# Sliding-window attention with key tiles shifted by half a tile

## The chip, the core and the metric

The kernel runs on one core of a Trainium2 chip: a matrix engine (TensorE, PE in the profile; its weight loads are PEld), a vector engine (VectorE, DVE), an activation engine (ScalarE, ACT), a general engine (GpSimd, POOL), a queue engine that issues DMAs (SyncE, SP), and 16 DMA engines. The metric is the device time of one execution in microseconds; lower is better.

## The reference

Two layers, each an attention block and a gated feed-forward block, on 2048 tokens of width 512, in bfloat16:

```python
def _A_ref(x, wqkv, wo):
    B, S, D = x.shape
    H = 32; Dh = D // H; W = 256
    qkv = (x @ wqkv).reshape(B, S, 3, H, Dh).transpose(2, 0, 3, 1, 4)
    q, k, v = qkv[0], qkv[1], qkv[2]
    scores = jnp.einsum("bhqd,bhkd->bhqk", q, k) * (Dh ** -0.5)
    idx = jnp.arange(S)
    mask = (idx[:, None] - idx[None, :] >= 0) & (idx[:, None] - idx[None, :] < W)
    scores = jnp.where(mask[None, None], scores, -1e9)
    p = _softmax(scores, axis=-1)
    o = jnp.einsum("bhqk,bhkd->bhqd", p, v)
    return o.transpose(0, 2, 1, 3).reshape(B, S, D) @ wo

def _B_ref(x, w_gate, w_up, w_down):          # widths 512, 1792
    return (_sigmoid(x @ w_gate) * (x @ w_up)) @ w_down

x = A_x
for _ in range(2):
    x = x + _A_ref(_layernorm(x), A_wqkv, A_wo)
    x = x + _B_ref(_layernorm(x), B_w_gate, B_w_up, B_w_down)
```

A query sees itself and the 255 tokens before it. There are 32 heads of 16 channels.

## The kernel before

**Layout and stages.** Tokens come in 16 tiles of 128 (`NT`), four to a group (`NBG`). For a tile: a layer norm on VectorE and POOL (`layer_norm`), a transpose into `xnT` (by TensorE for the first tiles, otherwise by a DMA), units of TensorE work for Q, K (a group at a time, `q_unit` L695, `k_unit` L726) and V (a tile at a time, `v_unit` L765), scores, exponentials, masks and values, a second transpose, the output projection (`oproj_unit` L889), and the feed-forward units (`glu_units` L790, `down_units` L851). The two layers run into each other: as soon as the tokens that a tile needs are there, its next stage may begin.

**The attention.** With a window of 256 and tiles of 128, the keys of a tile j concern six 64-token query units, 2j to 2j+5. The four in the middle are scored for all 128 keys (an A visit, four per tile, one for each eight heads: `scores` L1029, two quads of 256 columns). Of unit 2j only the first half of the keys counts, of 2j+5 only the second; a fifth visit R scores those two half-tile pieces (L1040, 8 quads of 64 columns; half as many for the last two tiles of a layer). The last tile has one S visit (L1050) in place of the A visits. Scores of a visit fill the four PSUM banks `Sps`; one exp on ScalarE empties them (L1082, 2048 columns) into `PTring` (nine 64-column units per head, placed by the table `UNIT`) or `edge`. VectorE multiplies the triangular pieces by a mask (L960).

The probabilities lie with the keys on the partitions. `values` (L1084) multiplies them with V, which carries a column of ones per head for the sum of the softmax: 32 output rows for each head, so that four heads (a quad of matmuls) share the 128 columns of the array. For a half tile (16 heads, one bank) and each of four columns of heads, a tile from t=2 on takes one quad of 128 columns from key tile t-1 and four quads of 64 columns: from t-2, from t, and from two copies `Vl` and `Vh` in which the half tiles of V for the edges stand next to each other, zero-padded to 128 rows (made by DMAs, `half_values` L1303). Rows of a token tile are stored interleaved (row 2k+z is token 64z+k), which the loads, the moves of Q and of the values, and the stores undo or make.

The result of a half is moved by VectorE or ScalarE from its bank to `OTs` (`after_values` L1115, L668), then transposed by a DMA to `Oq`, normalised, transposed again, and projected.

**The order.** It is written out ahead by a planner (`Plan`, L168), which replays a model of the chip and hands each engine its instructions in the order in which the model begins them. `pick` (L1206) decides what TensorE does next: a visit when its exp slot and its pace (`PACE`) allow it; values when all their masks, V and a free bank are there, and when TensorE is not in a dense run; otherwise `choose` (L1344) picks among the open dense units and the heads of the streams by `rank`. There are four free banks (`BANKS`) for dense units and values; `choose` keeps the last one free when the next values are due. A unit holds its bank until its eviction has run. VectorE and ScalarE tasks are taken by the priorities in `PRIO` and `LATE_PRIO`. An exp waits until the values that still read its ring units are done (`ring_free`, L930: the values of t-1, same half).

Of the kernel before, what the change touches and what calls it, by code (L numbers as in the profile page):

```python
# [12 lines left out]
P = 128  # L13
# [11 lines left out]
VW = H * VS + 32  # L25
UNITS = 9
# [8 lines left out]
UNIT = [  # L35
    (4, 5, 7, 8), (1, 2, 3, 4), (0, 1, 5, 6), (2, 3, 7, 8), (0, 1, 4, 5), (7, 2, 3, 6), (0, 1, 7, 8), (2, 3, 4, 5),
    (1, 2, 6, 7), (1, 3, 4, 0), (1, 2, 5, 6), (3, 4, 7, 8), (0, 1, 2, 3), (4, 5, 6, 7), (0, 1, 2), (8,),
    (3, 4, 5, 6), (0, 1, 7, 8), (2, 3, 4, 5), (1, 2, 6, 7), (1, 3, 4, 0), (1, 2, 5, 6), (3, 4, 7, 8), (1, 2, 3, 0),
    (4, 5, 6, 7), (1, 2, 3, 4), (0, 1, 5, 6), (2, 3, 7, 8), (0, 1, 4, 5), (2, 3, 6, 7), (0, 1, 2), (8,),
]  # L40


# [14 lines left out]
def pool_ns(n):  # L57
# [5 lines left out]
GLU = [[[1] * 4 + [4], [1] * 4 + [2] * 2, [1] * 6 + [2], [1] * 8, [2] * 4, [1] * 2 + [2] * 3, [2] * 2 + [4]], [[4] * 3 + [2, 1, 1], [4] * 3 + [2, 2], [4] * 4]]  # L63
PACE = [2682, 3207, 1600, 2511, 23.52]
EARLY = 12
# [16 lines left out]
PRIO = dict(st_x0=7.13, ap_x0=2.72, xt_x0=3.36, st_x1=-0.44, ap_x1=1.86, xt_x1=6.58, st_x=18.87, ap_x=6.56,  # L82
    xt_x=2.0, st_p=7.13, ap_p=4.46, xt_p=0.81, st_g=2.23, ap_g=1.32, xt_g=6.14, st_g0=5.97, ap_g0=3.21,
    xt_g0=1.33, tp=5.75, tp_g=-0.06, q=4.0, q0=5.51, q1=4.74, k=1.95, k0=-0.89, k1=-1.49, s=-1.15, s0=5.46,
    s1=3.28, v=0.28, v0=5.43, v1=14.72, vv=5.53, exp=3.64, exp0=4.71, m0=4.61, m00=-0.56, e0=1.11, e00=1.28,
    e1=7.21, e10=6.56, m2=0.64, m20=3.6, th=5.12, mu=-0.12, dn=1.29, add=-0.27, add0=1.8, out=-2.4, mv=5.8,
    mv0=6.23, oq=-2.27, oq0=-0.14, no=4.71, no0=2.61, on=5.93, on0=0.59, vc=9.2, vc0=-0.87)
OPT = dict(gu='SP', g1=1, bk=3, bq=2, wide=0, r0=2, g0=1, g2=1, x0=1, eps=1, hold=0, own=1, ck=0, cq=2,
    turn=2)
SLACK = dict(xt=1208, oq=843, on=211, vc=1208)  # L90
RANK = dict(tp=-1.708, o=-2, lead=14.747, far=7.411, v=9.3, g=1.778, d=1.823, feed=11.672, x3=21097, wd=474,
    go=364)
LATE_PRIO = dict(st_p=-0.04, ap_p=7.96, xt_p=-0.99, st_x=1.07, ap_x=4.81, xt_x=-1.16, st_g=1.75, ap_g=1.19,
    xt_g=2.76, q=3.84, k=4.33, s=4.05, v=0.61, exp=1.12, m0=4.62, e0=2.79, e1=4.39, m2=5.49, th=1.65, mu=2.51,
    dn=2.1, add=0.69, out=0.45, mv=3.49, oq=0.77, no=6.44, on=2.16, vc=0.22)
LATE_SLACK = dict(xt=489, oq=1327, on=2346, vc=897)
LATE_RANK = dict(tp=-2, o=1.576, lead=9.722, far=6.159, v=1.796, g=1.769, d=3.896, feed=7.551, go=1418)
# [271 lines left out]
class Net:  # L369


    def __init__(self, ctx, tc, A_x, wqkv, wo, w_gate, w_up, w_down, out):
# [24 lines left out]
        self.kTp = big.tile([P, NCQ, KS, 2, P], BF16, name="kTp")  # L397
        self.Vaug = [big.tile([P, 2, VW], BF16, name=f"Vaug{i}") for i in range(VP)]
        self.hT = big.tile([P, HCH * GW], BF16, name="hT")
        self.ring = big.tile([P, H, UNITS, HP], BF16, name="PTring")  # L400
        self.edge = big.tile([P, 5, H // 2, HP], BF16, name="edge")
        self.Vd = [[big.tile([P, 2, VW], BF16, name=f"V{'lh'[z]}{i}") for i in range(2)] for z in range(2)]
# [4 lines left out]
        self.odd = [big.tile([P, 1], F32, name=f"odd{z}") for z in range(2)]  # L407
# [9 lines left out]
        ring("xn", 2, [P, 2, D])  # L417
        ring("xnT", 3, [P, NBG, KT, P])
# [25 lines left out]
    def loads(self, A_x, wqkv, wo, w_gate, w_up, w_down):  # L444
# [12 lines left out]
        def load_x(dst, tiles, n, prio=2, queues=("SP", "SP"), after=0):  # L457
            done, parts = Event(), []
            for z in range(2):
                src = A_x[0].rearrange("(t z k) d -> z k t d", z=2, k=HP)[z][:, tiles, :]  # L460
                parts.append(load(dst[z:P:2], src, n * HP * D * 2, after, prio, queues[z], 780))
# [42 lines left out]
    def constants(self):  # L504
# [12 lines left out]
        for i in range(2):  # L517
            self.zeros(0, i)
# [1003 lines left out]
```

The softmax here doesn't subtract the row's maximum and nothing guards it: scores larger than these inputs give would overflow.

## Time and profile before

| what | us |
|---|---|
| median of 3 runs | 541.5 (540.59 to 541.67) |
| profiled execution, first to last instruction | 539.6 |
| dense matmuls of 512 columns of L862 (434) and L798 (560), mean of one | 0.380 |
| values L1109, matmuls of 64 columns (3840), mean of one | 0.193 |
| values L1109, matmuls of 128 columns (960), mean of one | 0.223 |
| exp L1082 on 2048 columns to PTring (114), mean of one | 1.881 |
| mask L960 (180), mean of one | 0.68 |
| copies Vl and Vh (60 DMAs of 68 KB), issue to landing | 2.4 and 2.5 |

A matmul's own duration is its passage through the pipeline, so the durations overlap: what one costs TensorE is the distance to the start of the next. The granted clock was full all through (0.999). In the timeline, a row names how many instructions of one kind were merged, its start and the time from the first one's start to the last one's end.

### The profile page before, as it was taken

To read this page: it belongs to the slowest core of one execution; us is meant where nothing else is said; L and a number is where in the kernel's file an instruction comes from. 1 tells how busy PE (TensorE), PEld (TensorE's weight loads), DVE (VectorE), ACT (ScalarE), POOL (GpSimd) and SP (SyncE) were. 2 spreads that over 40 slices of the span, in tenths; PEclk is the share of its full clock that TensorE was granted. 3 is DMA by queue.
4 is the path that set the end of the run, shared out by engine and by line. 5 is a ranking of instruction groups with operands and counts; after the bars stand their busy time and mean duration, and the time that the engine had idled before them with its cause. 6 is when DMAs were issued, how large, how long until landed. Compare 5 with 4: busy or idle time off the path is not lost.

```text
span 539.6 us, 21359 instructions
## 1 busy us (share of the span) xinstructions
PE 531.1 (98%) x9658; PEld 293.0 (54%) x9658; DVE 420.5 (78%) x844; ACT 382.3 (71%) x380; POOL 43.4 (8%) x99
## 2 busy tenths in 40 slices
PE   8999999999999999999999999999999999999997
PEld 8446755855767444544444444544444444455873
DVE  6999999789878997798977789778677785674442
ACT  4989989878888687776778767787667866540330
POOL 5301110001000110101100010101000000000000
PEclk9999999999999999999999999999999999999999
DMA  8890334232421323143110622117211241132001
GB/s 260 317 227 15 43 72 57 50 61 63 72 52 33 72 51 60 36 101 59 32 35 14 105 51 47 38 42 108 54 45 28 60 72 50 24 70 58 2 11 39
DMA packets 95067, 36.23 MB, mean 67 GB/s; under 512 B 78336, under 2 KB 93952, under 8 KB 94976
## 3 DMA queue, kind: packets, MB, share of 16 engines
q1 hardware_dynamic: 93600, 33.56, 29.9%
q8 instruction: 75, 1.23, 1.0%
q10 hardware_dynamic: 1376, 1.31, 0.8%
q14 instruction: 16, 0.13, 0.1%
HBM read 9.70 MB, written 2.10 MB: 22 GB/s over the span
## 4 chain that ended last, share of the span: by engine, by line
PE 89%; DVE 5%; ACT 2%; DMA 1%; issue 1%; POOL 0%; SPq 0%; ACTq 0%; POOLq 0%
PE bank L798 37%; PE bank L862 18%; PE bank L1109 9%; PE Sps L1029 7%; PE bank L893 5%; PE bank L734 4%; PE bank L770 3%; PE bank L703 3%; PE Sps L1040 2%; ACT PTring L1082 1%; DMA wq<-in_A_wqkv_dram 1%; DVE kTp L749 1%; DVE st L589 1%; DVE PTring L960 1%; DVE edge L960 1%
## 5 line engine op out<-in xcount | busy, mean ns | idle before, releaser
L1082 ACT ACTIVATE PTring<-Sps 128x2048 bf16<-128x2048 f32 (+1 forms) x122 | 226.0, 1852 | 63.2 <-PE Sps L1029 59.2
L798 PE MATMUL bank<-xnT,wu 128*128 128x512 bf16 (+2 forms) x728 | 128.2, 297 | 0.0
L798 PE MATMUL bank<-xnT,wg 128*128 128x512 bf16 (+2 forms) x728 | 128.2, 298 | 0.0
L862 PE MATMUL bank<-wd,hT 128*128 128x512 bf16 (+2 forms) x462 | 109.9, 373 | 0.0
L824 DVE SCALAR_TENSOR_TENSOR hT<-hT,bank 128x256 bf16<-128x256 bf16 (+1 forms) x154 | 80.8, 537 | 34.0 <-ACT hT L816 21.2
L816 ACT ACTIVATE hT<-bank 128x256 bf16<-128x256 f32 (+1 forms) x154 | 71.1, 482 | 48.5 <-PE bank L798 47.8
L798 PEld LDWEIGHTS <-wg 128*128 128x128 bf16 x728 | 60.7, 98 | 36.7 <-issue 2.3
L798 PEld LDWEIGHTS <-wu 128*128 128x128 bf16 x728 | 61.4, 98 | 34.5 <-issue 2.5
L1082 ACT ACTIVATE edge<-Sps 128x2048 bf16<-128x2048 f32 (+1 forms) x32 | 56.6, 1770 | 17.3 <-PE Sps L1040 17.3
L862 PEld LDWEIGHTS <-hT 128*128 128x128 bf16 x462 | 43.0, 98 | 46.4 <-issue 2.2
L668 DVE CAST OTs<-bank 128x512 bf16<-128x512 f32 x59 | 43.0, 729 | 21.5 <-PE bank L1109 21.1
L960 DVE TENSOR_TENSOR PTring<-PTring,mask 128x1024 bf16<-128x1024 bf16 x64 | 43.7, 684 | 12.3 <-ACT PTring L1082 12.1
L1109 PE MATMUL bank<-PTring,Vaug 128*32 128x64 bf16 (+1 forms) x2880 | 52.0, 203 | 0.0
L1109 PEld LDWEIGHTS <-Vaug 128*32 128x32 bf16 x2880 | 44.0, 97 | 12.0 <-issue 10.4
L1029 PE MATMUL Sps<-qT,kTp 32*128 32x256 bf16 (+3 forms) x1216 | 47.4, 248 | 1.2 <-ACT PTring L1082 1.1
L598 POOL TENSOR_SCALAR st<-st 128x2 f32<-128x2 f32 (+1 forms) x33 | 10.7, 325 | 443.6 <-DVE st L590 443.6
L589 DVE BATCH_NORM_STATS2 st<-xsb 128x6 f32<-128x512 bf16 x64 | 43.9, 686 | 1.7 <-DMA xsb<-in_A_x_dram 1.2
L1109 PE MATMUL bank<-edge,Vl 128*32 128x64 bf16 x1024 | 44.4, 193 | 0.1
L960 DVE TENSOR_TENSOR edge<-edge,maske 128x1024 bf16<-128x1024 bf16 x60 | 40.3, 682 | 3.4 <-ACT edge L1082 3.3
L1029 PEld LDWEIGHTS <-kTp 32*128 32x128 bf16 x1216 | 18.2, 92 | 45.4 <-issue 43.5
L1109 PE MATMUL bank<-edge,Vh 128*32 128x64 bf16 x896 | 40.8, 193 | 0.0
L960 DVE TENSOR_TENSOR PTring<-PTring,maskn 128x1024 bf16<-128x1024 bf16 x56 | 38.2, 682 | 0.0
(73 smaller groups left out, 522.0 us busy)
## 6 DMA issues: line engine op xcount, KB each, us to landing
Vl<-Vaug SPq DMA_DIRECT2D x32, 68.0 KB, 2.4
out_dram<-xsb SPq DMA_DIRECT2D x15, 128.0 KB, 2.1
Vh<-Vaug SPq DMA_DIRECT2D x28, 68.0 KB, 2.5
wg<-in_B_w_gate_dram SPq DMA_DIRECT2D x2, 896.0 KB, 9.7
wu<-in_B_w_up_dram SPq DMA_DIRECT2D x2, 896.0 KB
wd<-in_B_w_down_dram SPq DMA_DIRECT2D x7, 256.0 KB, 5.3
xsb<-in_A_x_dram SPq DMA_DIRECT2D x6, 256.0 KB, 7.4
wq<-in_A_wqkv_dram ACTq DMA_DIRECT2D x2, 256.0 KB, 4.5
```

Source lines behind the costliest of these rows:

```text
L589: nc.vector.bn_stats(out=st[:, 0:6], in_=self.xsb[:, t, :])
L668: self.nc.vector.tensor_copy(out=out, in_=in_)
L734: return [(mm_ns(w), lambda kt=kt, o=o: nc.tensor.matmul(self.banks[bank][:, o:o + w], lhsT=self.wq[:, kt, D + cq * P:D + cq * P + P], rhs ...
L798: return [(mm_ns(w), lambda i=i, j=j, fc=fc, wt=wt, kt=kt: self.nc.tensor.matmul(pt[:, i, j, :], lhsT=wt[:, kt, fc * P:(fc + 1) * P], rhs= ...
L816: self.nc.scalar.activation(out=self.hT[:, ch[0] * GW:ch[0] * GW + size], in_=pt, func=AF.Tanh, scale=0.5)
L824: self.nc.vector.scalar_tensor_tensor(out=h, in0=h, scalar=1.0, in1=pt, op0=ALU.add, op1=ALU.mult)
L862: nc.tensor.matmul(self.banks[bank][:, 0:w], lhsT=self.hT[:, at:at + P], rhs=self.wd[:, fc, d], start=fc == 0, stop=fc == FC - 1)
L893: return [(mm_ns(D), lambda c=c: nc.tensor.matmul(self.banks[bank][:], lhsT=b[0][:, c, :], rhs=self.wot[:, c, :], start=c == 0, stop=c == ...
L960: done = pl.task({"DVE": dve_bf_ns(1024)}, lambda e: nc.vector.tensor_tensor(out=r, in0=r, in1=m.to_broadcast([P, 16, HP]), op=ALU.mult), ...
L1029: nc.tensor.matmul(self.sps[:, m, o:o + n * HP], lhsT=kTp[32 * m:32 * m + 32, i, tt, e, :], rhs=self.qT[32 * m:32 * m + 32, i, q0:q0 + n * ...
L1082: nc.scalar.activation(out=out, in_=src, func=AF.Exp, scale=scale)
L1109: nc.tensor.matmul(o, lhsT=Va[:, c0:c0 + 32], rhs=p(h), start=k == 0 or t == 0, stop=k == len(parts) - 1 or t == 0, tile_position=(0, 32 * g))
```

## The change

Key tiles are shifted by 64 tokens against the query tiles: key tile t holds the tokens 128t-64 to 128t+63. An A visit then covers the query tiles t and t+1 whole, and values of a tile take key tile t and key tile t-1 as quads of 128 columns. What is left are two 64x64 edges per query tile: the second half of tile t against itself, and the first half against the 64 tokens that are 256 back. R scores these two edges with eight matmuls at a time (four row groups of 32 and two column halves of the array), with even heads in the upper half and odd heads in the lower half of the partitions. In `values` the edges are matmuls of 64 rows by 32 columns, even and odd heads in two row halves of the array and in two banks. Values of a tile are one block into two banks, the even heads in one and the odd heads in the other; it needs two free banks, and `choose` keeps two free.

The probabilities lie in five 128-column pairs per head (`PAIR`), and an exp waits for the values two tiles back. Tile 1 has no R visit (that of tile 0 makes both of their edges) and the last tile has two S visits. V units work on the shifted tiles: those of even tiles read a buffer `vx` that two POOL copies join from two half tiles, and that of the first tile in a group carries the last half tile of the group with it, so that it is evicted in two halves. `kTp` is a ring of 16 half tiles, and a K eviction that passes its end is cut in two. V copies are of 64 rows without padding. Rows are no longer interleaved, so loads, moves and stores are plain; `wo` comes in four loads with its rows in the new order of heads. The priorities, paces and ranks of the planner are other numbers.

```diff
 VS = 17
-VW = H * VS + 32
-UNITS = 9
+VN = H // 2 * VS
+VW = 2 * VN + 32
...
+def pair_slots():
+
+
+    out = []
+    for j in range(2 * NT):
+        held = set(out[-1]) if out else set()
+        held |= set(out[-2][1:]) if len(out) > 1 else set()
+        free = [p for p in range(PAIRS) if p not in held]
+        out.append(tuple(free[:1 if j % NT == NT - 1 else 2]))
+    return out
+
+
+PAIR = pair_slots()
...
-PACE = [2682, 3207, 1600, 2511, 23.52]
-EARLY = 12
+GLU = [[[1, 1, 1, 1, 4], [1, 1, 2, 1, 1, 2], [1, 1, 1, 1, 1, 1, 2], [1, 1, 1, 1, 1, 1, 1, 1], [2, 2, 2, 2], [1, 1, 2, 2, 2], [2, 2, 4]], [[4, 4, 4, 2, 2], [4, 4, 4, 2, 2], [4, 4, 4, 1, 1, 2]]]
+PACE = [2623.16, 2961.11, 2644.76, 1466.02, 27.75]
+EARLY = 4
...
-        self.kTp = big.tile([P, NCQ, KS, 2, P], BF16, name="kTp")
+        self.kTp = big.tile([P, NCQ, 2, 2 * KS, HP], BF16, name="kTp")
...
-        self.ring = big.tile([P, H, UNITS, HP], BF16, name="PTring")
-        self.edge = big.tile([P, 5, H // 2, HP], BF16, name="edge")
-        self.Vd = [[big.tile([P, 2, VW], BF16, name=f"V{'lh'[z]}{i}") for i in range(2)] for z in range(2)]
+        self.ring = big.tile([P, H, PAIRS, P], BF16, name="PTring")
+        self.edge = big.tile([P, 2, 2, H // 2, HP], BF16, name="edge")
+        self.Vd = [[big.tile([P, 2, VN + 32], BF16, name=f"V{'lh'[z]}{i}") for i in range(2)] for z in range(2)]
...
+        ring("vx", 2, [P, KT, 2, HP])
...
-        self.has_wo = load(self.wot[:], wo_src, D * D * 2)
+        self.has_wo = both([load(self.wot[:, 2 * e + k, :], wo_src[e, :, :, k, :], D * D // 2) for e in range(2) for k in range(2)])
...
+            at = (L * NT + t0) % KS * 2 + 1
+            cuts = [(0, 2 * n, at)] if at + 2 * n <= 2 * KS else [(0, 2 * n - 1, at), (2 * n - 1, 1, 0)]
...
+                for o, w, k in cuts:
+                    self.copy(e, self.kTp[:, cq, 0, k:k + w, :].rearrange("p u k -> p (u k)"), self.banks[u.bank][:, o * HP:(o + w) * HP])
...
-            needs.append(self.seen[divmod(gi * NBG + NBG - 1 - KS, NT)])
+            j = gi * NBG + NBG - 1 - KS
+            needs.append(self.seen[divmod(min(j + 2, j // NT * NT + NT - 1), NT)])
...
+        ahead, box = Event(), {}
+        if i % 2 == 0:
+            h = (i + 3) % NBG
+
+            def join(e):
+                box["vx"] = self.take("vx")
+                b, to = self.xnT[key][0], box["vx"][0]
+                nc.gpsimd.tensor_copy(out=to[:, :, 0, :], in_=b[:, h // 2, :, P + HP:2 * P])
+                nc.gpsimd.tensor_copy(out=to[:, :, 1, :], in_=b[:, i // 2, :, 0:HP])
+
+            ahead = pl.task({"POOL": 2 * pool_ns(KT * HP)}, join, [self.xn_ready[key, t], self.xn_ready[key, t - i + h]], 1, lambda: self.has("vx"), port=True).done
...
+            for half, k in ((slice(0, P), j),) if i else ((slice(HP, P), j), (slice(0, HP), j + 4)):
+                d = pl.task({"ACT": act_ns(D), "DVE": dve_ns(D)}, lambda e, half=half, k=k: self.copy(e, place(k, half), src[half]), [u.done] + self.v_free(k),
+                            self.prio["vv" if L == 0 and 2 <= t < 4 else "v" + self.phase(L, g)])
+                if half.start == 0:
+                    d.done.then(self.v_hi[L, t + 3 if i == 0 else t - 1].fire)
+                if half.stop == P:
+                    d.done.then(self.v_lo[L, t].fire)
+                done.append(d.done)
...
+                some = [(L, t, "A", cq) for cq in range(NCQ)] if t < NT - 1 else [(L, t, "S", h) for h in range(2)]
+                if t != 1:
+                    some.insert(min(OPT["r0"] if t else OPT["r1"], len(some)), (L, t, "R", 0))
+                self.visits += some
...
+        old = j - (1 if kind == "R" and t == 0 else 2)
+        if old >= 0:
+            deps.append(self.pv_done[divmod(old, NT)])
...
+        for z in range(2):
+            for cq in range(NCQ):
+                ku, qu = (2 * j + 2 * z + 1,) * 2 if t == 0 else (2 * j + 1,) * 2 if z == 0 else (2 * j - 4, 2 * j)
+                o = (z * NCQ + cq) * HP
+                for e in range(2):
+                    for m in range(4):
+                        mm(self.sps[e * HP:e * HP + HP, m, o:o + HP], m, self.kTp[32 * m:32 * m + 32, cq, e, (ku + 1) % (2 * KS), :],
+                           cq, qu, col=e * HP)
+        return pl.count(64) or 262
...
+        parts = [(j - k, PAIR[j - k][k]) for k in ((0, 1) if t else (0,))]
+        for e in range(2):
+            for col in range(4):
+                for k, pair in parts:
+                    V = self.Vaug[k // 2 % VP][:, k % 2, :]
+                    for g in range(4):
+                        c0 = VN * e + VS * (4 * col + g)
+                        nc.tensor.matmul(OT[e][32 * g:32 * g + 32, col, :], lhsT=V[:, c0:c0 + 32], rhs=self.ring[:, 8 * col + 2 * g + e, pair, :],
+                                         start=k == j and col == 0, stop=False, tile_position=(0, 32 * g))
...
+        edges = [(slice(HP, P), 0)] + [(slice(0, HP), 1)] * (t > 1)
...
+            for where, z in edges:
+                for e in range(2):
+                    r = slice(e * HP, e * HP + HP)
+                    for g in range(4):
+                        c0 = VS * (4 * col + g)
+                        nc.tensor.matmul(OT[e][32 * g:32 * g + 32, col, where], lhsT=self.vd[z, L, t - 2 * z][r, c0:c0 + 32],
+                                         rhs=self.edge[r, j % 2, z, 4 * g + col, :], start=False, stop=col == 3 and z == edges[-1][1], tile_position=(HP * e, 32 * g))
...
-        if self.pv_list and spare:
-            L, t, h = self.pv_list[0]
-            if len(self.masks[L, t, h]) == self.n_masks(t) and all(e.fired for e in self.masks[L, t, h]) and all(
-                    self.v_ready[L, jj].fired for jj in range(max(0, t - 2), t + 1)) and self.v_lo[L, t].fired and (
-                    t < 2 or self.v_hi[L, t - 2].fired):
+        if self.pv_list and len(spare) > 1:
+            L, t = self.pv_list[0]
+            if len(self.masks[L, t]) == self.n_masks(t) and all(e.fired for e in self.masks[L, t] + self.values_need(L, t)):
                 pv = self.pv_list[0]
...
+        banks = sorted(spare, key=lambda i: self.bank_turn[i])[:2]
+        for b in banks:
+            self.bank_user[b] = Unit(("v alues",), None, [], False, None)
+        end = pl.matmul("pv", self.values(*pv, banks))
...
-                if len(free) == 1:
+                late = sum(not e.fired for e in self.masks[k])
+                if len(free) <= (2 if late == 0 else 1 if late <= OPT["near"] else 0):
                     free = []
...
+        def blank(e):
+            nc.gpsimd.memset(self.Vaug[NT // 2 % VP][0:HP, 0, :], 0.0)
+
+        def restore(k):
+            V = self.Vaug[k // 2 % VP]
+            nc.gpsimd.memset(V[0:HP, k % 2, 0:VS * H].rearrange("p (h c) -> p h c", c=VS)[:, :, 16:VS], 1.0)
+
```

## The prediction

> **What bounds the kernel.** I read the page's busy times first, then its chain of waits, then what TensorE waited for.
>
> ```profile
> PE 531.1 (98%) x9658; PEld 293.0 (54%) x9658; DVE 420.5 (78%) x844; ACT 382.3 (71%) x380; POOL 43.4 (8%) x99
> PE 89%; DVE 5%; ACT 2%; DMA 1%; issue 1%; POOL 0%; SPq 0%; ACTq 0%; POOLq 0%
> ```
>
> TensorE is busy 98% of a 539.6 us span, 89% of the chain runs through it, and the waits charged to it sum to 4.6 us, all but 1.6 of them in the first 30 us. Between 180 and 480 us it has no idle time in a window table. So the time is the number of TensorE blocks times their lengths, plus a start and a tail. A busy TensorE is not one at its peak, so I price by the distance between the start of a block and the start of what follows, in the timeline:
>
> ```profile
> 243.34 0.40 PE L1029 MATMUL Sps<-qT,kTp 32*128 32x256 bf16 x8
> 243.66 0.21 PE L1109 MATMUL bank<-PTring,Vaug 128*32 128x64 bf16 x4
> ...
> 243.88 0.20 PE L1109 MATMUL bank<-edge,Vl 128*32 128x64 bf16 x4
> 244.01 0.39 PE L893 MATMUL bank<-wot,OnT 128*128 128x512 bf16 x1
> ```
>
> ```profile
> 269.40 0.38 PE L798 MATMUL bank<-xnT,wg 128*128 128x512 bf16 x1
> 269.71 0.40 PE L1029 MATMUL Sps<-qT,kTp 32*128 32x256 bf16 x8
> 270.04 0.27 PE L1109 MATMUL bank<-PTring,Vaug 128*32 128x128 bf16 x8
> 270.14 0.20 PE L1109 MATMUL bank<-edge,Vh 128*32 128x64 bf16 x4
> ...
> 270.71 0.20 PE L1109 MATMUL bank<-edge,Vl 128*32 128x64 bf16 x4
> 270.85 0.82 PE L798 MATMUL bank<-xnT,wg 128*128 128x512 bf16 x3
> ```
>
> ```profile
> 263.21 0.41 PE L1040 MATMUL Sps<-qT,kTp 32*128 32x64 bf16 x32
> 263.56 0.39 PE L770 MATMUL bank<-wq,xnT 128*128 128x512 bf16 x1
> ```
>
> Small matmuls go in fours ("quads") that run side by side in the array. Unrounded, a value block (half a tile) takes 351 ns at t=0 (8 quads of 64 columns), 574 at t=1 (4 quads of 128 and 8 of 64) and 808 from t=2 on (4 and 16); each is nearly the same in every instance. 808-574 is 8 quads of 64: **29.25 ns** each. 351-8x29.25 leaves **117 ns** for leaving the block; (574-117-234)/4 is **55.75 ns** for a quad of 128. The R block gives the same: 346 ns for 8 quads, 229 for the 4 of a half R, so 29.25 each and 112 around them. An A block takes 330 ns (two quads of 256 at 109, and 112). Going from a dense matmul into a block costs 96 more (312 ns to the next start, 216 otherwise).
>
> **The change, on TensorE.** Before, a tile from t=2 on takes two blocks: 2x808 = 1616 ns. The diff makes one block of 16 quads of 128 and 8 groups of eight matmuls: 64 rows by 32 columns, 64 columns moved, two row halves into two banks ("octets"). No octet is in this trace. Below: 64 columns of a 128-quad cost 27.9 ns. Above: eight matmuls as two quads one after the other, 58.5. I take **29.25**, since the starts inside a quad lie 3.6 to 3.8 ns apart, so eight can start within one 64-column quad. The change of tile shape inside the block is not in the trace either: nothing below, and above the 112 ns of leaving an A block, which a value block after it pays too (327 ns). I take 112.
>
> - t from 2 on: 892 + 234 + 117 + 112 = 1355, 261 less, 28 tiles: -7.3 us.
> - t=0: 446 + 117 + 229 = 792 against 702; t=1: 892 + 117 + 229 = 1238 against 1148; four tiles: +0.4.
> - R: 30 blocks of 8 octets at 346 (10.4 us) against 28x346 + 4x229 (10.6): -0.2.
> - A: 112 blocks at 330 and 8 split ones at 335 (4 quads of 128 and 112), 39.6 us, against 84x330 + 24x335 + 8x275 + 4x339 = 39.3: +0.3.
> - S: 4 blocks of 4x55.75+112 = 335 against 2x344: +0.65.
>
> The sum is **-6.2 us**. The number of dense matmuls stays: the V unit still makes four 512-column ones per tile, and the two GLU lists hold as many groups of one, two and four tiles. The profiled execution goes from 539.6 to 533.4 us; the median of the runs is 1.9 above that span, so I expect 535.3.
>
> All octets count 28x8+4x4 in values and 30x8 in R, 480: a nanosecond more in each is 0.48 us. At 58.5 ns they add 14.0 us, at 27.9 they take 0.6 off. The free inner switch takes 32x112 = 3.6 us off. So TensorE's sum lies between -10.4 and +7.9.
>
> The Trainium skill, "TensorEngine Tiling (Array Packing)", section Key Properties, speaks against the one block: changing the tiling mode drains the engine. It names no price; the 96 and 112 ns rows agree with it, and by the rule the gain is that with the full inner switch, without it the larger one. "TensorE: Matmul & The Clock Gate", section Measured speedup vs the span model, gives about 4 ns per further tile; by it an octet needs 32 ns and the sum would be 1.3 us worse, an estimate from that page.
>
> **The change off TensorE.** These I cost at nothing while TensorE is full.
>
> ```profile
> 120.00:180.00 60.00, 58.99 (x1392) 39.75 (x1391) 52.76 (x112) 50.65 (x56) 4.27 (x8) 1.00 0.31 57
> 180.00:240.00 60.00, 60.00 (x1151) 27.94 (x1149) 51.99 (x100) 45.09 (x40) 4.22 (x8) 1.00 0.30 60
> L668 DVE CAST OTs<-bank 128x512 bf16<-128x512 f32 x59 | 43.0, 729 | 21.5 <-PE bank L1109 21.1
> L668 DVE CAST qT<-bank 128x512 bf16<-128x512 f32 x15 | 10.0, 681 | 1.2 <-PE bank L703 1.1
> ```
>
> (Columns of the first two: window, length, busy PE, PEld, DVE, ACT, POOL, clock, DMA.) VectorE: the moves to OTs lose their reordering, 64x(729-681) = 3 us less at best; four more masks, 2.7 us; eight V evictions cut into two halves, up to 8x0.68 = 5.4; 16 K evictions with a second piece and two more splits, some 16x0.6 = 10 by the shortest rows (302 ns for a 128-column copy, 154 for a split). Together some 15 us more on 420. ScalarE: 154 full exps at 1.88 us are 289.5 us against 282.6 of before. Cover: 120 and 157 us idle; between 120 and 180 us VectorE has 7 us of 60 left, and from 20 to 60 only 1.5 of 40:
>
> ```profile
> 20.00:60.00 40.00, 38.93 (x755) 21.92 (x755) 38.50 (x85) 37.56 (x38) 6.23 (x12) 1.00 0.50 126
> ```
>
> There the chain of waits runs mostly through VectorE. In that stage fall four of the cut K evictions (2.4 us) and two halves of V (1.4); against them the masks are made in five small copies instead of eight operations, 0.9 us for 2.8, and eight moves are 0.05 shorter: net +1.5 us. I take nothing, as TensorE has Q, K and V of later groups to fill with; uncovered it is 1.5.
>
> POOL gets 32 copies of half tiles (16 V units wait for theirs). No such copy is in the trace; between a 206 ns memset of 128x128 and a 773 ns power, 7 to 25 us on an engine 8% busy. First V units start at 17.4 us, first values at 29.5, and a copy of 0.4 to 1.5 us fits between. The wait is on the V unit alone, and choose takes another unit from the streams. On SP the V copies become 64 from 60 (0.60 us each to issue) and wo four loads for one (0.81): some 2 us later for the x of tiles 8 to 11, gate and up weights, which are queued behind it at 6 us and first used after 40. The first half's values now wait for the whole tile's masks, some 6 us more (two visits of 3.2, as the A blocks at 266.47 and 269.71); behind them stand only the two moves and the transposes to Oq, which needed both halves before too. K of a group waits until the R block of two tiles later has read its old keys; ten visits, some 30 us, remain to refill four K units. Exp of tile j waits for the values of j-2 instead of j-1: a wait loosened, worth nothing here, as the waits of TensorE on an exp sum to 1.1 us.
>
> **Rivals.** *Starved of banks (slower).* A value block now takes two of four banks at once, and both are freed only when two moves of 0.73 us have run, nearly all on VectorE (59 of 64); choose also keeps two free ahead of it. Two banks with four-matmul units last 2x0.864 = 1.73 us. If a mask (0.68) stands with the moves (1.46), the first unit's eviction ends at 2.14+0.7 = 2.84: a stall of 1.1 us. At a third of 32 tiles that is 12 us: 547. It decides against the change from 6.2/32 = 0.19 us per tile on. For it: VectorE at 88% in layer 0. Against: ScalarE can evict too, and one down unit of 14x0.216 = 3.0 us covers it all, as does an A or R block between.
>
> *Octets don't run side by side (slower).* The two row halves follow each other: +7.9, 549. For it: no 64-row tile appears in this trace, and 16 instructions in 29 ns is twice the sustained rate of a 64-column quad (8 in 29). Against: starts 3.6 ns apart. It would mean that the 64-row packing does nothing. It decides from 29.25+6.2/0.48 = 42 ns.
>
> *The switch is cheap and the ring's extra tile of slack lets blocks go where they fit (faster still).* -6.2-3.6 = -9.8: 531.7. For it: between them the R and value blocks lost 1.4 us over their multiples of the block lengths before (one R of 990 ns, one value block of 1056), which a looser order may spare. Against: every shape change in the trace costs about 100 ns.
>
> **How the numbers follow.** The forecast has 0.50, the greater gain 0.22, starved banks 0.18, serial octets 0.10. The two on the faster side make 0.72; banks that stall less than the gain add a little: faster 0.73, within 0.2% (1.1 us, about what can be told from no change) 0.05, slower 0.22. For the range I go below the greater gain's 531.7 by the spare 1.4 us, to 530.3, and up to where starved banks mostly end, 546. The forecast's own range is 532 to 538.
>
> **What would show it.** One value block per tile of about 1.36 us from t=2 on, R blocks still near 346 ns, TensorE's busy time about 6 us lower, no new waits. A value block of 1.59 us or R of 580 shows serial octets; TensorE idle ahead of dense matmuls, ended by an eviction, shows starved banks. Wrong altogether would be idle time at the start or at the layers' seam, where V of tile 0 now waits for the group's last tile and a blank on POOL, of over 6 us.

## The result and the profile after

The changed kernel takes 556.1 us (median of 4 runs, 554.5 to 559.1) against 541.4 for the kernel before: 1.028 times as long, 95% interval 1.025 to 1.031. The forecast was 535.3 us, with a range up to 546.0; the time lies outside it, on the other side of no change.

The profiled execution is the 559.1 us one; its span is 557.4 us. From its page, TensorE's busy time and the chain of waits:

```profile
PE 538.9 (97%) x9473; PEld 300.1 (54%) x9538; DVE 419.8 (75%) x875; ACT 397.8 (71%) x407; POOL 54.7 (10%) x127
PE 89%; DVE 4%; DMA 3%; issue 2%; ACT 1%; ACTq 0%; POOL 0%; DVEq 0%
```

TensorE bounds the kernel as before, and is busy 7.8 us longer where 6 us less were forecast. (65 of its matmul records are missing, so a few block ends in the trace lie one dense matmul too late; the lengths below are medians.) The timeline shows a value block of the changed kernel, its R block, and the dense matmul after each:

```profile
362.10 1.08 PE L1080 MATMUL bank<-PTring,Vaug 128*32 128x128 bf16 x64
363.11 0.23 PE L1089 MATMUL bank<-edge,Vl 64*32 64x64 bf16 x8
363.15 0.21 PE L1089 MATMUL bank<-edge,Vh 64*32 64x64 bf16 x8
363.18 0.22 PE L1089 MATMUL bank<-edge,Vl 64*32 64x64 bf16 x8
363.21 0.22 PE L1089 MATMUL bank<-edge,Vh 64*32 64x64 bf16 x8
363.34 0.26 PE L1089 MATMUL bank<-edge,Vl 64*32 64x64 bf16 x8
363.40 0.26 PE L1089 MATMUL bank<-edge,Vh 64*32 64x64 bf16 x8
363.47 0.26 PE L1089 MATMUL bank<-edge,Vl 64*32 64x64 bf16 x8
363.54 0.26 PE L1089 MATMUL bank<-edge,Vh 64*32 64x64 bf16 x8
363.73 1.04 PE L945 MATMUL bank<-wot,OnT 128*128 128x512 bf16 x3
...
368.15 0.71 PE L1021 MATMUL Sps<-qT,kTp 32*64 32x64 bf16 x64
368.79 1.04 PE L850 MATMUL bank<-xnT,wu 128*128 128x512 bf16 x4
```

Each row of eight is one octet. The first four start some 30 ns apart, as forecast. Then 130 ns pass, and the other four start 67 ns apart. The block's quads take 1.01 us, its octets 0.616 and the whole 1.62 us, where 1.355 was forecast; R takes 0.64 us instead of 0.346. Quads, the inner change of shape (1008 = 892 + 116 ns), A (330) and split A and S (335) are as priced.

The single starts of the octet part at 363.1 us, in ns between one matmul and the next (a weight load stands before each):

```
matmuls 1 to 32:   4 3 3 4 3 3 4 15 5 3 3 2 6 1 5 4 6 2 3 2 6 2 5 3 6 2 4 1 6 2 5
32 to 33:          104
matmuls 33 to 64:  7 9 9 8 9 8 8 9 8 8 9 8 8 9 8 8 9 8 8 9 8 8 9 8 8 9 8 8 9 8 8
```

The second half goes at 8.33 ns per matmul, with the load exactly between two: one instruction each 4.17 ns. R looks the same: 32 matmuls in a burst, that is 64 instructions, then a gap of 100 ns (72 in two of the 30 blocks), then 8.33 ns.

VectorE and the evictions gave nothing to explain. From the windows (length, busy PE, PEld, DVE, ACT, POOL, clock, DMA) and the groups:

```profile
20.00:60.00 40.00, 35.20 (x603) 20.57 (x605) 33.96 (x83) 33.53 (x38) 10.38 (x21) 0.96 0.60 170
120.00:180.00 60.00, 58.96 (x1402) 41.19 (x1408) 49.63 (x116) 52.50 (x62) 4.64 (x10) 1.00 0.33 56
180.00:240.00 60.00, 59.05 (x1254) 30.23 (x1260) 51.34 (x100) 49.04 (x42) 5.29 (x9) 1.00 0.31 57
L678 DVE CAST OTs<-bank 128x512 bf16<-128x512 f32 x34 | 23.1, 688 | 21.9 <-PE bank L1089 21.7
```

The moves to OTs take 688 ns instead of 729, and ScalarE took 30 of the 64. What is new outside the blocks lies early: between 20 and 60 us TensorE is busy 35.2 us instead of 38.9. Waits of TensorE from its list:

```profile
PE bank L1089 <- DMA Vl<-Vaug: 2.8, 1, 2.8
PE Sps L1021 <- ACT PTring L1066: 2.3, 4, 1.0
PE bank L1089 <- issue: 1.9, 1, 1.9
...
PE bank L1154 <- DVE OTs L678: 0.2, 1, 0.2
```

The first values wait 2.8 us for the copy `Vl`; within another value block 1.9 us pass in which TensorE waits for nothing that the profile names. An eviction to OTs holds it up for 0.2 us in all.

### The profile page after: what moved, and what is told of

It is laid out like the page before. It is cut to its first block, busy times and chain, and to the rows that moved or that the text cites. A ratio compares the mean times of both kernels' runs of the same rounds, so it can differ in the third digit from the quotient of the medians.

```text
span 557.4 us, 21171 instructions
## 1 busy us (share of the span) xinstructions
PE 538.9 (97%) x9473; PEld 300.1 (54%) x9538; DVE 419.8 (75%) x875; ACT 397.8 (71%) x407; POOL 54.7 (10%) x127
## 4 chain that ended last, share of the span: by engine, by line
PE 89%; DVE 4%; DMA 3%; issue 2%; ACT 1%; ACTq 0%; POOL 0%; DVEq 0%
PE bank L850 35%; PE bank L914 17%; PE Sps L1021 10%; PE bank L1080 5%; PE bank L743 5%; PE bank L945 4%; PE bank L713 4%; PE bank L801 4%; PE bank L1089 3%; DMA Vl<-Vaug 2%; ACT edge L1066 1%; DMA wq<-in_A_wqkv_dram 1%; DVE kTp L760 1%; DVE st L590 1%; DVE Vaug L678 0%
## 5 line engine op out<-in xcount | busy, mean ns | idle before, releaser
L1066 ACT ACTIVATE PTring<-Sps 128x2048 bf16<-128x2048 f32 x124 | 233.0, 1879 | 41.8 <-PE Sps L1021 40.9
L914 PE MATMUL bank<-wd,hT 128*128 128x512 bf16 (+2 forms) x433 | 104.5, 373 | 2.6 <-issue 1.7
L850 PEld LDWEIGHTS <-wg 128*128 128x128 bf16 x728 | 62.0, 99 | 38.9 <-issue 3.3
L1021 PE MATMUL Sps<-qT,kTp 32*64 32x64 bf16 (+2 forms) x3008 | 70.7, 224 | 2.6 <-ACT PTring L1066 2.3
L1066 ACT ACTIVATE edge<-Sps 128x2048 bf16<-128x2048 f32 x30 | 56.3, 1877 | 22.1 <-PE Sps L1021 19.7
L1021 PEld LDWEIGHTS <-kTp 32*64 32x64 bf16 (+1 forms) x3008 | 34.2, 99 | 54.7 <-issue 52.0
L923 DVE SCALAR_TENSOR_TENSOR xsb<-bank,xsb 128x512 bf16<-128x512 f32 (+2 forms) x33 | 22.1, 669 | 26.5 <-PE bank L914 25.6
L678 DVE CAST OTs<-bank 128x512 bf16<-128x512 f32 x34 | 23.1, 688 | 21.9 <-PE bank L1089 21.7
L1080 PE MATMUL bank<-PTring,Vaug 128*32 128x128 bf16 x1984 | 33.9, 220 | 0.2 <-DVE PTring L993 0.2
L743 PE MATMUL bank<-xnT,wq 128*128 128x512 bf16 (+1 forms) x164 | 33.5, 342 | 0.4 <-DMA wq<-in_A_wqkv_dram 0.3
L1080 PEld LDWEIGHTS <-Vaug 128*32 128x32 bf16 x1984 | 28.2, 97 | 9.3 <-issue 8.6
```

Source lines behind the costliest of these rows:

```text
L678: self.nc.vector.tensor_copy(out=out, in_=in_)
L743: return [(mm_ns(w), lambda kt=kt, o=o: nc.tensor.matmul(self.banks[bank][:, o:o + w], lhsT=self.wq[:, kt, D + cq * P:D + cq * P + P], rhs ...
L850: return [(mm_ns(w), lambda i=i, j=j, fc=fc, wt=wt, kt=kt: self.nc.tensor.matmul(pt[:, i, j, :], lhsT=wt[:, kt, fc * P:(fc + 1) * P], rhs= ...
L914: nc.tensor.matmul(self.banks[bank][:, 0:w], lhsT=self.hT[:, at:at + P], rhs=self.wd[:, fc, d], start=fc == 0, stop=fc == FC - 1)
L1021: nc.tensor.matmul(out, lhsT=keys, rhs=self.qT[32 * m:32 * m + 32, cq, q0:q0 + n * HP], start=True, stop=True, tile_position=(32 * m, col))
L1066: nc.scalar.activation(out=out, in_=src, func=AF.Exp, scale=1.0 / float(np.sqrt(DH)))
```

## The experiments

Letters in the expectations: **F**, the feed: TensorE is handed instructions at a limited rate, so a block of many small matmuls costs by their number. **S**, serial octets: the array itself runs the two halves of an octet one after the other, so it costs by columns. **O**, the planner's too low prices for these blocks put the order wrong. **W**, waits and order hold the time, not the blocks. **L**, the late first loads. **P**, the planner's numbers fit only the one order they were chosen for.

### Half the columns in each octet of R

```diff
-mm(self.sps[e*HP:e*HP+HP, m, o:o+HP], m, kTp[...], cq, qu, col=e*HP)
+nc.tensor.matmul(self.sps[e*HP:e*HP+HP, m, o:o+HP//2], lhsT=kTp[...],
+                 rhs=self.qT[32*m:32*m+32, cq, q0:q0+HP//2], ...)
```

> The changed kernel, but each matmul of an R visit moves 32 query columns instead of 64 (half of the edge scores is left out, so the probabilities of the edges are not the reference's). Theory F (feed): TensorE has about 28 pairs of weight load and matmul in stock when an R block begins, and gets each further pair only every 8.33 ns; then the columns do not matter, an R block stays at 630 to 640 ns and the time stays at 555 us within 2. Rival S (array): the two column halves of an octet follow each other in the array, 2 x 64 columns; with half the columns an octet falls from 66 to about 33 ns, an R block to about 376 ns, and 30 blocks take 7.9 us less.

Measured: 555.2 us, ratio to before 1.025 [1.023, 1.027]. R goes from 639 to 612 ns, though half its columns are gone (27 ns less, where F had none); its second half still starts a matmul each 8.33 ns. Serial halves would make it 376. S falls.

### The values in two parts, with a pause between the octets

```diff
+for part in range(2):                    # columns of heads 0-1, then 2-3
+    quads of 128 for these columns
+    octets for these columns
-quads of 128 for all four columns
-octets for all four columns
```

> The changed kernel with the same matmuls in the value block in another order: the 128-column quads of two columns of heads, their four octets, then the other two columns and their four octets. Two more changes of tile shape inside the block, some 110 ns each. Theory F (feed): 32 pairs are little more than the stock, so four octets take about 128 ns instead of 250, and the whole block from t=2 on is 892 + 256 + 336 + 117 = 1600 ns, against 1624 now: time the same within 2 us. Rival S (array): the octets still take 62 ns each, the block 892 + 500 + 336 + 117 = 1845, and 28 blocks add 6 us.

Measured: 557.9 us, 1.032 [1.028, 1.036]. The octets, now 32 matmuls at a time, take 242 and 244 ns instead of 616 for 64. Less some 115 for leaving, four octets take 128, 32 each: the forecast's price, while they are no more than 32. Two more changes of shape (each part of quads is 562 ns long: 446 and 116) eat the gain: 1.61 us for the whole, as F had it. The same 64 matmuls cost 616-117 = 499 ns in one row and 2x128 in two, which a price by columns can't give.

### The planner told of the real lengths

```diff
-return pl.count(64) or 262
+return pl.count(64) or 527
-len(parts) * 8 * 57 + len(edges) * 4 * 31 + SWITCH
+len(parts) * 8 * 57 + len(edges) * 4 * 62 + SWITCH
```

> The changed kernel, but the planner that writes the order is told the measured lengths: 527 for an R block (262 before) and 62 for an octet of values (31). Block lengths on the chip must stay at 639 and 1008+616 ns under every theory. Rival O (order): some 4 us of the 15 that block lengths do not explain come from an order written for shorter blocks; then the time falls to about 551. Without it the time stays at 555 within 2.

Measured: 562.9 us, 1.039 [1.036, 1.043]. The blocks keep their lengths (616 and 639 ns); the order laid on the true lengths is some 7 us slower than that laid on the wrong ones. So O falls as far as this one order tells. In its trace TensorE stands still four times without a named cause, 4.9 us together where the kernel after has 1.9; the last section tells what these gaps are.

### Quads in place of octets, in R and in the values

K holds the two heads of a pair next to each other, and the copies of V are padded to 128 rows (one buffer each), so that an edge is a quad of 64 columns again.

```diff
-for e in range(2):
-    for m in range(4):
-        mm(self.sps[e*HP:e*HP+HP, m, o:o+HP], m, kTp[.., cq, e, unit, :], cq, qu, col=e*HP)
+for m in range(4):
+    mm(self.sps[:, m, o:o+HP], m, kTp[.., cq, u*P:u*P+P], cq, qu)
...
-lhsT=self.vd[z, L, t-2*z][r, c0:c0+32], rhs=self.edge[r, ...], tile_position=(HP*e, 32*g)
+lhsT=self.vd[z, L, t-2*z][:, c0:c0+32], rhs=self.edge[:, ...], tile_position=(0, 32*g)
```

> The shift and the 128-column value quads stay, the octets go: R in quads with 128 columns of weights (32 matmuls for 64), edges of values as quads of 128 rows with zero-padded V, in between the 128-column quads, so no change of tile shape in the block. For it K lies with the two heads of a pair next to each other, and the padded V copies have one buffer instead of two. The planner keeps its prices. Theories F and S both: R blocks 346 ns (293 less, 30 of them: 8.8 us), value blocks from t=2 on 892 + 468 + 117 = 1477 (147 less, 28 of them: 4.1 us), time about 542. If the time stays above 550, most of the loss is not in the octets.

Measured: 558.9 us, 1.033 [1.030, 1.035]. R is 345 ns and the value block 1477, as expected, and TensorE is busy 527.3 us instead of 538.9. The time did not follow: the planner made another order out of it, with one V copy fewer in stock and K splits of 473 ns instead of 330. Its windows and the waits of TensorE in that trace:

```profile
120.00:180.00 60.00, 54.57 (x1132) 38.12 (x1129) 49.55 (x112) 50.48 (x57) 2.92 (x5) 0.97 0.26 45
180.00:240.00 60.00, 55.17 (x1216) 29.06 (x1214) 53.49 (x102) 52.13 (x43) 7.51 (x12) 1.00 0.37 66
```

```profile
PE Sps L1023 <- ACT PTring L1067: 6.1, 11, 1.8
PE bank L947 <- DMA OnT<-On: 2.1, 2, 1.1
```

TensorE idles 10 us between 120 and 240 us. In the whole trace, 3.4 us of its idle time are four gaps of the kind told in the last section. An expectation that changes the order along with the blocks could not be kept; the next runs hold the order.

### Octets in R of the kernel before

```diff
-for m in range(4):
-    matmul(self.sps[:, m, o:o+HP], lhsT=both heads of kTp[.., tt], tile_position=(32*m, 0))
+for e in range(2):
+    for m in range(4):
+        matmul(self.sps[e*HP:e*HP+HP, m, o:o+HP], lhsT=kTp[.., tt, e, z:P:2], tile_position=(32*m, e*HP))
```

> The kernel before, in its own order, with one part of the change alone: each quad of an R visit with 128 columns of weights becomes eight matmuls of 64 columns of weights (64 pairs of load and matmul for 32). Theory F (feed): its 28 full R blocks grow from 346 to 639 ns, 8.2 us, and the time to about 550. Rival W (other waits cover it): TensorE's blocks grow, but the time by less than half of that, below 545.5.

Measured: 555.1 us, 1.026 [1.024, 1.027]: +14.0 us from this part of the change alone, in the order of before. 28 R blocks are 641 ns instead of 346 (+8.3), the four halved ones, 32 matmuls each, 264 instead of 229. The rest is next to the blocks: the distances from a dense matmul to the next one sum to 3.1 us more (a wait of 1.4 for `OnT`, 0.9 for `xnT`), and the values, which were not touched, have a gap at 488.8 us:

```profile
488.54 0.24 PE L1110 MATMUL bank<-PTring,Vaug 128*32 128x128 bf16 x3
490.36 0.22 PE L1110 MATMUL bank<-PTring,Vaug 128*32 128x128 bf16 x4 [1.59 <-issue]
```

### Quads in R alone, in the order of after

K as `[unit, head of the pair, key]`, so that R's quad reads 128 adjacent columns; an A visit then needs two 64-column weight halves for each quad. The order is that of the changed kernel.

```diff
-self.kTp[..., cq, 2, 2*KS, HP]
+self.kTp[..., cq, 2*KS, 2, HP]
-for m in range(4): mm(sps[:, m, ..], m, full(m, i, e), ...)
+for y in range(2):
+    for m in range(4): mm(sps[y*HP:y*HP+HP, m, ..], m, kTp[.., unit+y, e, :], ..., y*HP)
```

> The changed kernel in its own order, with R in quads: 128 columns of weights, 32 pairs of load and matmul for 64. For that K lies by 64-token units with the even and odd heads' halves next to each other, and an A visit loads its weights as two 64-column halves (16 pairs for 8, 256 columns moved, well within the stock). Theory F: R blocks 346 instead of 639 ns, A blocks stay at 330, 30 x 293 ns = 8.8 us less, time about 546.7. Rival W: TensorE comes earlier to waits that the longer blocks covered, and less than half arrives: time above 551.

Measured: 558.9 us (555.7 to 559.3), 1.032 [1.029, 1.034]. R is 345 ns, 8.8 us less in 30 blocks; A is 357 instead of 330, 3.3 us more; and three gaps in value blocks, none of them in the kernel after, took 4.0 us. One of them:

```profile
174.68 0.24 PE L1085 MATMUL bank<-edge,Vh 64*32 64x64 bf16 x6
176.90 0.20 PE L1085 MATMUL bank<-edge,Vh 64*32 64x64 bf16 x2 [1.99 <-issue]
```

The expectation of 546.7 us missed. The traced execution is the fastest, 555.7 us; its span lies 3.4 us under that of the kernel after, which is what -8.8, +3.3, +4.0 and the missing 1.9 us gap of that kernel add up to; the match is not exact, as the granted clock was 0.997 here and 0.994 there. The other three executions took 558.8 to 559.3 us at a clock of 0.991. What the gaps are is told in the last section.

### Half the octets of the values, in the order of after

```diff
-for col in range(4):
+for col in range(2, 4):
     for where, z in edges:
```

> The changed kernel in its own order, with half of the octets in values left out (the edges of half of the heads are missing from the result): 32 pairs for 64. Theory F: the octet part of a value block falls from 616 to 244 ns, 372 x 28 = 10.4 us, time about 545. If octets cost by their columns (S) it falls by half of 500, 250 x 28 = 7.0 us, time 548.5. Rival W: less than half of the gain arrives, time above 550.

Measured: 546.5 us, 1.009 [1.007, 1.011], 9.6 us under the changed kernel. The octet part is 244 ns instead of 616: halving the matmuls takes 60% of it. 28x372 = 10.4 us, and nearly all of it arrives in the time.

### Both: quads in R, and half the octets of the values

> The two before together, with half of the octets in values left out (the edges of half of the heads are missing from the result): R 346 ns, value blocks 1252 ns from t=2 on, so TensorE has about as much to do as the forecast had it, less 3 us. Theory F alone: 19 us less, time about 536. Rival W: the order leaves TensorE waiting in between, time above 545; between 536 and 545 both.

Measured: 540.0 us, 0.999 [0.997, 1.001]. From the kernel after: -10.4 (values), -8.8 (R), +3.3 (A), together -15.9; measured -16.2. The timeline of a value block and of an A block:

```profile
363.35 1.08 PE L1076 MATMUL bank<-PTring,Vaug 128*32 128x128 bf16 x64
364.36 0.22 PE L1085 MATMUL bank<-edge,Vl 64*32 64x64 bf16 x8
364.39 0.21 PE L1085 MATMUL bank<-edge,Vh 64*32 64x64 bf16 x8
364.42 0.21 PE L1085 MATMUL bank<-edge,Vl 64*32 64x64 bf16 x8
364.45 0.21 PE L1085 MATMUL bank<-edge,Vh 64*32 64x64 bf16 x8
364.60 0.44 PE L1021 MATMUL Sps<-qT,kTp 32*64 32x256 bf16 x16
364.97 1.25 PE L713 MATMUL bank<-xnT,wq 128*128 128x512 bf16 x5
```

Four octets, each 30 ns after the last, and the next block 0.15 us after them: the pause and the slow half are gone. From the kernel after on, with an order that stands still, the time follows the lengths of TensorE's blocks. The 540.0 lies between the expectation's marks of 536 and 545, and 3.3 of the 4 us over 536 are the A blocks; so W falls. Against the kernel before, the blocks alone would give 535.1 (worked out in the second expectation under the loads of wo): 4.8 us are not in them.

### The loads of wo last

```diff
-four loads of wo ahead of those of the gate and up weights
+the same four, issued after the last of these
```

> The changed kernel in its own order, but the four loads of wo are issued after the gate and up weights instead of ahead of x of tiles 8 to 11 (the planner still thinks them at the old place). Theory L (loads): the four loads made the start late, gate began at 13.8 us instead of 9.2 and only 203 GB/s flowed from 10 to 20 us instead of 360 to 400; so the copies of V came behind them and the first values waited 2.3 to 3.5 us, after which the clock fell. Then the wait is gone or under 1 us, and the time is 3 to 5 us less than the 555.5 of the changed kernel. Rival: the wait goes, but the next one (a mask, an exp) takes its place: time within 1.5 us of 555.5.

Measured: 554.1 us, 1.022 [1.021, 1.024], 2 us under the changed kernel, short of the 3 to 5 expected. The wait for `Vl` is gone, but others take part of its place (1.9 us for `wq`). The stretch from 10 to 20 us of before, after and this one (last two columns: DMA share and GB/s):

```profile
10.00:20.00 10.00, 9.42 (x111) 6.17 (x109) 9.05 (x24) 9.00 (x15) 4.72 (x18) 1.00 1.06 384
```

```profile
10.00:20.00 10.00, 8.60 (x106) 5.72 (x107) 7.72 (x23) 8.32 (x12) 4.64 (x15) 1.00 1.04 204
```

```profile
10.00:20.00 10.00, 10.00 (x119) 7.87 (x117) 4.98 (x16) 6.13 (x10) 3.84 (x14) 0.83 1.08 301
```

The engines of the DMAs are full in all three, and move half as much in the kernel after, where 136 packets of 3.5 KB fall in the stretch instead of 681. This trace lacks no record, so its sums stand beside those of before, by the distance from each matmul to the next: scores 60.7 us against 51.6, values 52.3 against 49.7, dense 437.4 against 433.3. L holds for 2 us at most. And part of that is the clock: at a granted clock of 1.000 three executions took 553.7 to 554.2 us, and two of the changed kernel 554.5 and 555.1. The same edit on the kernel with quads in R and half the octets:

> R in quads and half of the octets in values left out (the edges of half of the heads are missing from the result), as once before at 540.0, with the loads of wo last. Block lengths of that kernel, worked out against the kernel before, give 541.0 - 6.2 - 2.9 (value blocks 1252 for 1355) + 3.2 (A blocks 357 for 330) = 535.1. Theory L: the 4.8 us that it lies above that are the late start, and the time falls to 535 to 537. Rival: they are elsewhere, and it stays within 1.5 us of 540.

Measured: 538.3 us, 0.994 [0.992, 0.995], 1.7 us under its partner and over the 535 to 537 of L. All four executions had a clock of 1.000; the six of the partner at 0.999 and more took 538.4 to 540.0 us, the four at 0.996 and 0.997 took 541.5 to 542.8. So most of the 1.7 is the clock, and 3.2 us over the 535.1 stay without a cause.

### Quads, planned with their real lengths

```diff
-return pl.count(64) or 262
+return pl.count(32) or 244
-len(edges) * 4 * 31 + SWITCH
+len(edges) * 8 * 29
-"DVE": 620 - 140 * (NBG - n) + 220 * more
+"DVE": 1100 - 140 * (NBG - n) + 220 * more
```

> The kernel without octets (R and edges in quads, shift kept), and the planner is told its lengths: 244 for R, 29 for each edge quad, 1100 for the two splits of K on VectorE (620 before), since they write every second element. TensorE's blocks are 13 us shorter than in the changed kernel (R 345, value blocks 1477). Theory P (the order is only as good as its numbers, which were found for another kernel): block lengths as said, and the time stays above 548, with TensorE idle ahead of dense matmuls. Rival: the 559 of that kernel came from wrong prices alone; then the time falls to 545 or below.

Measured: 552.3 us, 1.019 [1.017, 1.021]. R 345 and values 1477 ns once more, TensorE busy 531.9 us, and still 10.5 us over before. In its trace:

```profile
PE Sps L1024 <- ACT PTring L1068: 7.1, 11, 1.8
PE Sps L1024 <- issue: 2.1, 3, 1.2
```

And with the priorities, paces and ranks of the kernel before in place of those of the change:

> The same kernel without octets, with right prices, and the planner's priorities, ranks and paces of the kernel before in place of the new ones. Under theory P both sets of numbers were found for other kernels and the time stays above 548. If the new numbers were a part of the loss, the time is at least 4 us below that of the same kernel with the new numbers; at 538.8 the shift alone would give what its blocks save, 2.7 us.

Measured: 559.3 us, 1.032 [1.030, 1.034]; waits of 9.9 us on an exp and 5.3 without a named cause (four gaps, see the last section). Neither set of numbers serves the kernel with quads, as P expected; that a set found for it would do better, no run shows. No whole version beats the kernel before.

## Why the prediction was wrong

**The step that failed** is the price of an octet: "I take **29.25**, since the starts inside a quad lie 3.6 to 3.8 ns apart, so eight can start within one 64-column quad". They can, and do: 30 ns each, for the first four. The step took the spacing of a burst for a rate that lasts. After some 64 instructions TensorE gets one instruction each 4.17 ns, so an octet of 16 takes 67 ns, with 64 columns or with 32. Over a block it comes to (616-117)/8 = 62.4 ns in the values and (639-112)/8 = 65.9 in R: 30x293 + 28x265 ns = 16.2 us above the forecast. The sum's -6.2 becomes +10.0.

**The row that would have shown it** stood in the trace of before. There a value block from t=2 on has 80 pairs of a load and a matmul in 808-117 = 691 ns, 8.6 ns each, hardly above the limit of 8.33. An R block had 32 pairs, just the stock. No block ran 64 pairs at half that distance, as the change asks. The rival of serial octets saw it: "16 instructions in 29 ns is twice the sustained rate of a 64-column quad (8 in 29)". Its upper bound of 58.5 ns was within 13% of the truth, its time of 549 nearer than the forecast, and it got a chance of 0.10. Its mechanism was wrong: the halves do run side by side, and with half the columns R got 27 ns shorter, not 263. And the bound was too low: two quads in a row was taken as the dearest case.

**The Trainium skill's** "TensorE: Matmul & The Clock Gate", section Measured speedup vs the span model, puts a further tile at about 4 ns. The trace shows that for 32 matmuls, and 8.33 after. Its opening table gives TensorE's queue a depth of 64; the 32 pairs of the burst are 64 instructions.

**What else held and what did not.** The inner change of shape cost 116 ns (112 taken), A 330, S and split A 335, the moves to OTs 688 ns. VectorE was to gain 15 us of work and has 0.7 less, ScalarE 15.5 more instead of 6.9: evictions went to ScalarE. POOL's 11.3 more lie in the 7 to 25. Starved banks did not come: 0.2 us of waits on OTs. The loads, "some 2 us later", were 3.7 to 4.6 us later (up weights at 15.0 us against 11.3, gate weights at 13.8 against 9.2); the start, taken as nothing, cost some 2 us by the run that puts `wo` last, part of it clock. The 1.9 us gap in a block was in no step. The trace of before had one of the same kind, of 0.46 us: it is in the R block of 990 ns, which the prediction thought that a looser order may spare (its lines stand in the last section).

**The sum.** +10.0 from the blocks, 1.9 from the gap and 2.8 from the wait for `Vl` make 14.7, and the medians differ by 14.7. Part of this agreement is luck: gap and wait were read from the execution of 559.1 us, whose span lies 17.8 us over that of before. Most of the 3.1 us left there is the clock, for which the prediction had no term. Two windows of that trace, the first after the wait for `Vl`, the second after the gap (third column from the end: the granted clock):

```profile
33.70:37.20 3.50, 3.50 (x19) 1.83 (x16) 2.77 (x8) 2.31 (x2) 0.94 (x2) 0.51 0.91 235
67.90:71.30 3.40, 3.27 (x80) 2.80 (x80) 1.33 (x3) 2.44 (x3) 0.00 (x0) 0.50 0.58 111
```

At half the clock each loses some 1.7 us, an estimate; in the trace of before the clock is full up to 535 us. The four executions of the changed kernel go by the clock: 554.5 and 555.1 us at 1.000, 557.1 at 0.997, 559.1 at 0.994. Putting `wo` last took the 2.8 away and won 2.0. In the trace of that run, scores stand 9.1 us above those of before and values 2.6 (1.7 of it a gap), which are the blocks and the gap; dense matmuls stand 4.1 above, which no step foresaw. Part of this is the clock, 0.83 from 10 to 20 us.

**Open.** Whether the shifted tiles pay with quads in an order made for them: from t=2 on their one block takes 1477 ns where before took 2x808, 28x139 = 3.9 us less, but all three orders tried lost more than that. Quads in both places in the very order of after were not tried. Nor is it shown in full why each new order loses 7 us (the one on true prices) to 17 us (quads, 559 against the 542 that their blocks gave to expect) on the chip that the planner's model doesn't see. A part of it are the gaps of the last section: 4.9 us in the order on true prices, 3.4 and 5.3 in the two runs with quads at 559, against 1.9 in the kernel after.

## What to carry to other kernels

Count the instructions of a block of small matmuls, loads included, and not only its columns: up to 64 in a row went at about 2 ns each here, and beyond that at 4.17, so splitting each matmul into two that run side by side nearly doubled the price of the R block (639 ns for 346). The spacing seen within four matmuls is the pace of a burst; ask what a row of the trace shows over as many instructions as the changed block will have. And to learn what a block is worth, change it in an order that stands still: a planner that lays a new order moved the time by 7 to 17 us, as much as the blocks.

## What the runs showed of the hardware

**The pace of TensorE's instructions**: 4.17 ns each after about 64, with 64-column and 32-column matmuls alike, and after a pause of 72 to 107 ns in the kernel after. Every matmul here has a load of its own, so no run tells a limit on instructions from one on loads. Why nothing is refilled during the burst, no run shows. 0.56 us of 128-column quads are enough to have the next 32 pairs fast again.

**Instructions come in blocks, and a block can be late.** The page of the kernel after lists a DMA queue of its own for them (packets, MB, share):

```profile
q8 instruction: 74, 1.21, 0.9%
```

That is 16 KB a packet, and 74 times 256 is 18944, close to the 19076 loads and matmuls of TensorE. In all fourteen traces, each gap of over 0.3 us ahead of a matmul that no wait explains (28 of them, from 10 us on) ends 1.2 to 1.8 us after such a packet has landed. Packets of this queue that landed in a gap or at its start, from the traces, with the number of TensorE's instructions (loads and matmuls) begun by then:

```
kernel                  gap starts at   packet starts, lands   begun at landing   goes on at
after                   66.16           65.60  66.52            1977               68.03
octets in R of before   488.78          487.96 488.84          20407              490.36
quads in R              174.92          174.68 175.63           7101              176.90
quads in R              157.21          156.08 157.16           6333              158.44
half columns in R       64.77           63.93  64.92            1977               66.26
quads, planned          144.29          142.89 144.12           5051               145.49
quads, old numbers      76.24           75.88  76.75            2491               78.17
quads, old numbers      172.86          172.60 173.54           6331               174.91
```

Within each gap no instruction begins, and its number is the one at which TensorE stood still. In these rows it goes on 1.3 to 1.5 us after the packet has landed. These numbers differ by multiples of 256 up to a few (each leaves 183 to 189 when divided by 256). Two packets never start less than 3.2 us apart in any of the traces, and 256 instructions at 4.17 ns last 1.07 us: where an R block, a value block and short dense matmuls come together, TensorE would run out. That is a reading of these traces; no run took a gap away by a thinner stretch alone.

Octets are not needed for it: the last three rows are of kernels without any, and the kernel before has one gap, in an R block of quads, 1.36 us after a packet has landed:

```profile
140.14 0.38 PE L1040 MATMUL Sps<-qT,kTp 32*128 32x64 bf16 x27
140.99 0.22 PE L1040 MATMUL Sps<-qT,kTp 32*128 32x64 bf16 x5 [0.46 <-issue]
```

With half the octets in the values, the longest ahead of a matmul is 0.4 us.

The Trainium skill's "Runtime: NRT & Kernel Launch", section Instruction fetch mechanics, says that instructions are refilled in 16 KiB blocks of 256 and that the cost is mostly hidden; the packets and the 256 agree, but hidden it is not here, with 1.9 us lost in the kernel after, 4.0 in the values of the one with quads in R and 5.3 in the one with the old numbers.

**64-column weights**: an A block with two weight halves a quad took 357 ns instead of 330, with the same columns moved.
